# One head per 2 MB tile in place of two heads per 4 MB tile, in an attention-gradient kernel at the DMA limit

## The chip, the cores and the metric

The kernel runs on one core of one Trainium2 chip. The metric is the device time of the whole program in microseconds (us), lower is better; a time quoted here is the median of a kernel's runs, with the lowest and highest in brackets. The core computes with five engines: TensorE (PE, matrix products; its weight loads are counted apart as PEld), VectorE (DVE), ScalarE (ACT), GpSimd (POOL) and SyncE (SP). Its data travels through 16 DMA engines between the main memory (HBM) and the on-chip memory.

 "Same" means within 2%.

## The reference

For each of 64 heads (2 batches of 32) there is one query row of 128 numbers and 8192 rows of K and V; all data is bf16. The outputs are the attention output and the three gradients:

```python
B, H, Sq, Sk, D = 2, 32, 1, 8192, 128
def _fwd_reference(q, k, v):
    scale = q.shape[-1] ** -0.5
    scores = jnp.einsum("bhqd,bhkd->bhqk", q, k) * scale
    p = _softmax(scores, axis=-1)
    return jnp.einsum("bhqk,bhkd->bhqd", p, v)

def reference(q, k, v, grad_out):
    out, vjp = jax.vjp(_fwd_reference, q, k, v)
    return (out, *vjp(grad_out))            # out, dq, dk, dv
```

K and V of one head are 2 MB each, so 268.4 MB must be read. The gradients dK and dV have the same shapes, so 268.4 MB must be written. All other data is tiny.

## The kernel before

The kernel keeps six 4 MB tiles, each holding K or V of two heads. A tile has 128 partitions of 128 rows, which is 32 KB per partition. `load` fills a tile with one DMA of 4 MB. The program then advances in slots; in a slot a sixteen-row chunk of a tile is transposed on PE, copied to on-chip memory by ACT, and used for scores on PE. Later slots form the products with the weights (`acc`) and the gradient (`outer`). A gradient is written over the tile it came from, and is stored by one DMA of 4 MB when the last chunk is done; the last pair is stored in smaller pieces.

```python
GH = 2                                   # heads in a tile
NTILE = 6
...
    NT = GH * Sk // P                    # 128 rows in a partition
    NCH = NT // CH                       # 8 chunks in a tile
    SL = 2 * NCH                         # 16 slots for a pair of heads
    load_eng = nc.sync
    store_eng = nc.gpsimd
...
    def load(i, w, pieces=(NCH,)):
        t = kvp.tile([P, NT, D], BF16, tag=f"kv{slot_of(i, w)}", name="kvt")
        src = (v_v if w else k_v)[i]
        c = 0
        for m in pieces:
            n0, n1 = c * CH, (c + m) * CH
            pin(load_eng.dma_start(out=t[:, n0:n1, :], in_=src[:, n0:n1, :]))
            c += m
...
    def outer(i, w, c, ends):            # gradient of one chunk, in place
        pin(nc.vector.tensor_tensor(out=h.tile[w][:, n0 : n0 + CH, :] ..., op=ALU.mult))
        if c + 1 in ends:
            at = ends.index(c + 1)
            b0, b1 = (ends[at - 1] if at else 0) * CH, (c + 1) * CH
            dst = (dv_v if w else dk_v)[i]
            pin(store_eng.dma_start(out=dst[:, b0:b1, :], in_=h.tile[w][:, b0:b1, :]))

    A1 = NCH + 4; O1 = A1 + 1; A0 = A1 + NCH; O0 = A0 + 1
    whole = [NCH]
    last_v = [NCH // 2, NCH]
    last_k = [NCH // 2, NCH - 2, NCH - 1, NCH]
    for g in range(SL * NP + O0 + NCH + 4 - SL):
        if (i := at(O1 + NCH)) is not None and i + 3 < NP:
            load(i + 3, 0)
        if (i := at(O0 + NCH)) is not None and i + 3 < NP:
            load(i + 3, 1)
        if x := within(O1):
            outer(x[0], 1, x[1], last_v if x[0] == NP - 1 else whole)
        ...
            ev = transpose_chunk(i, r)   # 16 transposes on PE, one copy on ACT
        ...
            score_chunk(*prev)           # 16 score products on PE
```

The cuts are marked with `...`.

## Time and profile before

| before | value | where it is read |
|---|---|---|
| time | 1307.86 us (1306.82 to 1308.02), 3 runs | the timed runs |
| profiled span | 1310.5 us | first line of the page |
| PE / ACT / DVE busy | 88% / 75% / 65% | first part of the page |
| loads + stores, share of the DMA engines | 49.5% + 48.2% | queue table |
| rate at 200–400 us, at 600–800 us | 427, 413 GB/s | windows |

These lines are from the profile page of the kernel before: the busy time of each engine with its instruction count, the mean busy share of the 16 DMA engines (in tenths) and the rate they moved in 40 equal slices of the span, the DMA queues (packets, MB, share of 16 engines' span), and two kinds of DMA with the median time from issue to landing in us. Loads are q1 and stores are q0.

```profile
PE 1147.5 (88%) x19108; PEld 849.1 (65%) x19108; DVE 850.5 (65%) x1551; ACT 984.3 (75%) x641; POOL 37.4 (3%) x76
...
DMA  9999999999999999999999999999999999999968
GB/s 399 429 374 429 427 429 427 429 428 428 427 424 417 429 422 421 413 415 418 414 413 412 411 417 420 413 417 419 403 421 411 421 408 414 425 404 423 414 257 348
...
q1 hardware_dynamic: 9968, 268.51, 49.5%
q0 software_dynamic: 9792, 268.44, 48.2%
q8 instruction: 149, 2.44, 0.7%
...
out_dram<-kvt POOLq DMA_DIRECT2D x62, 4096.0 KB, 40.2
kvt<-in_v_dram SPq DMA_DIRECT2D x32, 4096.0 KB, 27.8
```

The DMA row is nine tenths or more for 38 of 40 slices while no computing engine is full. The kernel is bound by DMA. The rate is 427 to 429 GB/s at first and about 415 in the second half, at the same busy share.

The windows view of before says it by stretch. Columns: the stretch, its length, busy us of PE, PEld, DVE, ACT and POOL with instruction counts, the granted PE clock, the DMA share and the rate in GB/s.

```profile
60.00:100.00 40.00, 40.00 (x725) 30.01 (x721) 30.90 (x55) 36.72 (x24) 1.06 (x2) 1.00 0.93 384
200.00:400.00 200.00, 178.63 (x2968) 132.21 (x2965) 131.99 (x239) 152.75 (x100) 5.32 (x10) 0.92 1.00 427
600.00:800.00 200.00, 178.48 (x2933) 131.79 (x2929) 129.54 (x236) 150.99 (x99) 4.78 (x9) 0.91 1.00 413
...
1260.00:1270.00 10.00, 8.87 (x129) 6.62 (x131) 3.52 (x7) 6.03 (x5) 0.00 (x0) 0.83 0.33 139
1270.00:1280.00 10.00, 9.93 (x176) 7.10 (x172) 9.28 (x16) 9.50 (x8) 0.53 (x1) 1.00 0.51 215
```

### The profile page before, as it was taken

To read this page: it belongs to the slowest core of one execution; us is meant where nothing else is said; L and a number is where in the kernel's file an instruction comes from. 1 tells how busy PE (TensorE), PEld (TensorE's weight loads), DVE (VectorE), ACT (ScalarE), POOL (GpSimd) and SP (SyncE) were. 2 spreads that over 40 slices of the span, in tenths; PEclk is the share of its full clock that TensorE was granted. 3 is DMA by queue.
4 is the path that set the end of the run, shared out by engine and by line. 5 is a ranking of instruction groups with operands and counts; after the bars stand their busy time and mean duration, and the time that the engine had idled before them with its cause. 6 is when DMAs were issued, how large, how long until landed. Compare 5 with 4: busy or idle time off the path is not lost.

```text
span 1310.5 us, 41375 instructions
## 1 busy us (share of the span) xinstructions
PE 1147.5 (88%) x19108; PEld 849.1 (65%) x19108; DVE 850.5 (65%) x1551; ACT 984.3 (75%) x641; POOL 37.4 (3%) x76
## 2 busy tenths in 40 slices
PE   5999998898988988989889898898998988888894
PEld 4777766676766666666666676666666666666661
DVE  0677875766766767657676675665766757566666
ACT  5999987876877877778777787777876878777770
POOL 0000000000000000000000000000000000000000
PEclk9999998998989989889898898988988989888896
DMA  9999999999999999999999999999999999999968
GB/s 399 429 374 429 427 429 427 429 428 428 427 424 417 429 422 421 413 415 418 414 413 412 411 417 420 413 417 419 403 421 411 421 408 414 425 404 423 414 257 348
DMA packets 19933, 539.58 MB, mean 412 GB/s; under 512 B 2480, under 2 KB 2480, under 8 KB 2992
## 3 DMA queue, kind: packets, MB, share of 16 engines
q1 hardware_dynamic: 9968, 268.51, 49.5%
q0 software_dynamic: 9792, 268.44, 48.2%
q8 instruction: 149, 2.44, 0.7%
q14 instruction: 24, 0.20, 0.0%
HBM read 268.47 MB, written 268.47 MB: 410 GB/s over the span
## 4 chain that ended last, share of the span: by engine, by line
issue 78%; DMA 14%; PE 3%; POOL 2%; DVE 1%; SPq 0%; POOLq 0%; ACT 0%; DVEq 0%; ACTq 0%
DMA kvt<-in_v_dram 11%; DMA out_dram<-kvt 3%; POOL out_dram L446 2%; PE tp L183 1%; DVE kvt L432 1%; PE acc L376 1%; PE dpw L194 1%; POOLq L446 0%; PE sw L194 0%; ACT ev L185 0%; DVE sel L399 0%; SPq L93 0%; SPq L100 0%; PE sw L222 0%; PE acc L413 0%
## 5 line engine op out<-in xcount | busy, mean ns | idle before, releaser
L185 ACT COPY ev<-tp 128x2048 bf16<-128x2048 bf16 x512 | 954.0, 1865 | 293.6 <-PE tp L183 276.1
L183 PE MATMUL tp<-ident_bf,kvt 128*128 128x128 bf16 x8192 | 585.3, 229 | 127.3 <-DMA kvt<-in_k_dram 76.8
L432 DVE TENSOR_TENSOR kvt<-qb,pair 128x2048 bf16<-128x2048 bf16 x512 | 615.3, 1219 | 49.6 <-PE acc L376 46.7
L183 PEld LDWEIGHTS <-kvt 128*128 128x128 bf16 x8192 | 505.1, 103 | 137.2 <-DMA kvt<-in_k_dram 79.1
L194 PEld LDWEIGHTS <-ev 128*128 128x128 bf16 x8192 | 239.9, 96 | 218.0 <-issue 135.4
L376 PE MATMUL acc<-kvt,E_pad 128*64 128x512 bf16 x1024 | 173.1, 421 | 0.0
L376 PE MATMUL acc<-kvt,dS_pad 128*64 128x512 bf16 x1024 | 169.4, 416 | 1.0 <-DVE dS_pad L362 1.0
L194 PE MATMUL sw<-qdT,ev 128*128 128x2 bf16 x4096 | 142.0, 164 | 2.2 <-ACT ev L185 2.2
L194 PE MATMUL dpw<-qdT,ev 128*128 128x2 bf16 x4096 | 142.2, 164 | 1.0 <-ACT ev L185 1.0
L270 DVE CUSTOM_DVE_ANT_0 junk<-E_f,dpw 64x128 bf16<-64x128 f32 x64 | 18.3, 285 | 144.1 <-PE dpw L194 143.7
L207 DVE TENSOR_REDUCE mp<-sw 64x1 f32<-64x128 f32 x64 | 18.5, 289 | 108.5 <-PE sw L194 108.1
L446 POOL DMA_DIRECT2D out_dram<-kvt x68 | 36.3, 534 | 1261.7 <-DVE kvt L432 632.9
L399 DVE SCALAR_TENSOR_TENSOR sel<-acc,diag,sel 128x128 f32<-128x128 f32 x192 | 67.3, 351 | 6.8
L376 PEld LDWEIGHTS <-dS_pad 128*64 128x64 bf16 x1024 | 38.2, 112 | 29.4 <-issue 6.3
L376 PEld LDWEIGHTS <-E_pad 128*64 128x64 bf16 x1024 | 37.7, 112 | 26.8 <-issue 6.5
L262 DVE CAST E_pad<-E_f 64x128 bf16<-64x128 f32 x64 | 15.3, 239 | 48.5 <-ACT E_f L252 48.5
L413 PE MATMUL acc<-par,sel 128*128 128x2 f32 x128 | 22.0, 241 | 8.0 <-DVE sel L399 8.0
L176 DVE CAST qb<-dpw 128x128 bf16<-128x128 f32 x64 | 18.2, 284 | 13.4 <-PE dpw L167 13.4
L413 PEld LDWEIGHTS acc<-par,sel 128*128 128x128 f32 x128 | 19.7, 195 | 9.5 <-DVE sel L399 9.5
L340 DVE TENSOR_SCALAR negdelta<-dpw,rl 128x1 f32<-128x1 f32 x32 | 7.0, 218 | 27.0 <-PE dpw L300 27.0
L252 ACT ACTIVATE E_f<-sw,negm 64x128 f32<-64x128 f32 x64 | 23.2, 362 | 1.6
L352 DVE SCALAR_TENSOR_TENSOR dSu<-dpw,negdelta,E_f 64x128 f32<-64x128 f32 x64 | 22.4, 350 | 2.1
(49 smaller groups left out, 230.1 us busy)
## 6 DMA issues: line engine op xcount, KB each, us to landing
out_dram<-kvt POOLq DMA_DIRECT2D x62, 4096.0 KB, 40.2
kvt<-in_v_dram SPq DMA_DIRECT2D x32, 4096.0 KB, 27.8
kvt<-in_k_dram SPq DMA_DIRECT2D x31, 4096.0 KB, 27.9
out_dram<-kvt POOLq DMA_DIRECT2D x3, 2048.0 KB, 8.7
kvt<-in_k_dram SPq DMA_DIRECT2D x1, 2048.0 KB, 11.5
kvt<-in_k_dram SPq DMA_DIRECT2D x2, 512.0 KB, 4.5
kvt<-in_k_dram SPq DMA_DIRECT2D x1, 1024.0 KB, 6.9
out_dram<-kvt POOLq DMA_DIRECT2D x1, 1024.0 KB, 7.6
```

Of the source, the lines that this page charges most:

```text
L183: pin(nc.tensor.transpose(tp[:, t, :], src[:, c * CH + t, :], ident_bf[:]))
L185: pin(nc.scalar.copy(out=ev[:], in_=tp[:]))
L194: nc.tensor.matmul(dst[:, c * CH + t, :], lhsT=ev[:, t, :], rhs=qdT[:, w, GH * i : GH * (i + 1)], start=True, stop=True,)
L207: pin(nc.vector.reduce_max(out=h.mp[hs], in_=h.s[hs, :, g], axis=AX.X))
L252: nc.scalar.activation(out=h.E_f[hs], in_=h.s[hs, :, g], func=ACT.Exp, bias=h.negm[hs], scale=scale, accum_out=h.ld[hs, g : g + 1],)
L270: nc.vector.tensor_tensor_reduce(out=junk[hs], in0=h.E_f[hs], in1=h.dp[hs, :, g], scale=1.0, scalar=0.0, op0=ALU.mult, op1=ALU.add, accum_ ...
L352: nc.vector.scalar_tensor_tensor(out=dSu[hs], in0=h.dp[hs, :, g], scalar=negdelta[hs], in1=h.E_f[hs], op0=ALU.add, op1=ALU.mult,)
L376: nc.tensor.matmul(h.acc[w][g : g + CW, :], lhsT=wts[:, n0 * GH : n0 * GH + CW], rhs=rows[:, n0 : n0 + QT, :].rearrange("p n d -> p (n d)" ...
L399: nc.vector.scalar_tensor_tensor(out=h.sel[:], in0=block, scalar=diag[:, b : b + 1], in1=h.sel[:], op0=ALU.mult, op1=ALU.add,)
L413: nc.tensor.matmul(h.acc[w][:, 0:GH], lhsT=h.sel[:], rhs=par[:], start=True, stop=True)
L432: nc.vector.tensor_tensor(out=h.tile[w][:, n0 : n0 + CH, :].rearrange("p n (e t) -> p n e t", t=2), in0=h.qb[w][:] .rearrange("p (e t) -> ...
L446: pin(store_eng.dma_start(out=dst[:, b0:b1, :], in_=h.tile[w][:, b0:b1, :]))
```

## The change

A tile holds one head (2 MB, 16 KB per partition), and there are twelve. A head takes 8 slots where a pair took 16, so a head's steps are half as wide and come twice as often. Gradients are written over the tile as before. The first store can go out earlier, transfers are finer, and the last head is stored chunk by chunk. The intent is a shorter fill, a shorter tail and a deeper supply of tiles for the DMA engines. The core of the diff, with cuts marked:

```diff
-GH = 2
-NTILE = 6
+NTILE = 12
...
-    NT = GH * Sk // P
+    NT = Sk // P
...
-    load(0, 0, (1, 1, 2, 4))
+    load(0, 0, (1, 1, 2))
...
-        for g, hs in halves:
-            pin(nc.vector.reduce_max(out=h.mp[hs], in_=h.s[hs, :, g], axis=AX.X))
+        pin(nc.vector.reduce_max(out=h.mp[:], in_=h.s, axis=AX.X))
...      (exponential, weighing and normalising likewise: once per head, no halves)
-                    lhsT=wts[:, n0 * GH : n0 * GH + CW],
+                    lhsT=wts[:, n0 : n0 + CW],
...
-    last_v = [NCH // 2, NCH]
-    last_k = [NCH // 2, NCH - 2, NCH - 1, NCH]
+    last = list(range(1, NCH + 1))
+    AHEAD = NTILE // 2
...
-        if (i := at(O1 + NCH)) is not None and i + 3 < NP:
-            load(i + 3, 0)
+        if (i := at(O1 + NCH)) is not None and i + AHEAD < BH:
+            load(i + AHEAD, 0)
...
-            outer(x[0], 1, x[1], last_v if x[0] == NP - 1 else whole)
+            outer(x[0], 1, x[1], last if x[0] == BH - 1 else whole)
```

## The prediction

> **What bounds the kernel now.** The DMA engines. The page's DMA row is 9 in every slice but the last two; its queue table gives loads 49.5% and stores 48.2% of 16 engines' span. PE is busy 88%, ACT 75%, DVE 65%. While it had prefetched tiles (window 60 to 100 us) PE ran 725 matmuls in 40 us, against 2940 in 200 us later: compute can go about a fifth faster than it is fed. The Trainium skill (DMA: Bandwidth & Descriptors, "Issuing engines are not separate DMA queues") says that queues share the same 16 engines and interleave; the trace agrees, the shares sum to 98%.
>
> My account of one DMA engine's 1310 us, from the packet records:
> - 1024 packets of 32 KB at the median 1213 ns: 1242 us
> - instruction fetch (0.7%): 9 us
> - semaphore packets of 9 ns: 1 us
> - packets slower than the median: about 25 us in loads, 8 in stores, nearly all after 400 us, in the first third of a load, on several engines at once; the windows show 427 GB/s at 200 to 400 us and 413 to 419 later
> - idle: about 18 us in the last 70 us (windows 1260 to 1280: share 0.33 and 0.51; after 1300: 0.59), 3 at the start, 3 around 70 to 80 us (202 and 328 GB/s).
>
> **What the change does.**
> 1. A tile row is 16 KB. The 16 KB packets that exist take 611 ns (loads), so twice 611 less 1213 is 9 ns per 32 KB: +9 us, and +1 for twice the semaphore packets.
> 2. Tail. Now the last load lands about 1261 us, 12.6 MB of stores are left from 1274, and the end comes 50 us after the landing. After, 6.3 MB remain, the last head has half the slots and its stores go out by chunk: 9 to 10 us of idle in place of 18, -8 us. Last landing to end falls to about 35 us.
> 3. Fill. First store near 30 us instead of 55.6; the dip at 70 to 80 us goes: -3 us.
> 4. PE and ACT work is equal (about 80 more matmuls of 19108). DVE gets twice the picks (+90 us at 351 ns each) and half-width softmax steps, off the critical path. A head holds its tiles for 17 and 9 slots of 4 per tile, not 29 and 14 of 8 per tile, so 18 MB are free for transfers in place of 13. DMA is saturated already, so this buys little.
> 5. Twice as many loads begin. If each beginning costs what it does now (25 us over 64 loads), slow packets grow by up to 25 us; if the deeper queue keeps loads back to back, as before 400 us, they shrink. I put +5 us.
>
> Sum: 1308 + 10 - 8 - 3 + 5 = 1312 us. Range 1288 to 1336. Faster by over 2%: 0.07; within 2%: 0.86; slower by over 2%: 0.07.
>
> **What would show it.** DMA row at 9 to the end; median 16 KB packet about 611 ns; load and store shares near 98%; last 70 us with about 10 us of idle; no slice under 400 GB/s at 60 to 100 us; DVE 900 to 950 us, PE and ACT about unchanged; stores over 20 us to landing (queue, not compute).
>
> **What would make it wrong.** Slow packets vanishing (towards 1280) or doubling (1335); per-head chains (maximum, exponential, normalisation, twice as often) stalling PE enough to starve the DMA, seen as DMA share below 0.97 in the middle; 2 MB stores paying a start-up that 4 MB ones hid.

## More of the kernel before

A run has a state. A run over 1.5% above the fastest run of the same kernel is called slow and left out; everything compared here is fast against fast.

The mean share counts an engine as busy when a packet of its is under way, however long that packet takes.

## The result, and the profile after

The kernel after took 1304.59 us (1303.87 to 1304.87, 4 runs), and the kernel before, on the same chip in the same rounds, 1307.94 us (1306.82 to 1308.81, 4 runs). The ratio is 0.9974, 95% interval 0.9957 to 0.9991, which is "same". All ratios here are the mean time of one kernel's fast runs over the mean of the other's in the same rounds, so not quite the ratio of the quoted medians. The predicted 1312 us was 7 us too high and well inside the range. The sum was right; the next sections show that two of its terms had the wrong sign.

The same lines of the page, for the kernel after (span 1303.1 us):

```profile
PE 1154.0 (89%) x19268; PEld 873.0 (67%) x19268; DVE 937.5 (72%) x2122; ACT 974.8 (75%) x641; POOL 72.4 (6%) x142
...
DMA  9999999999999999999999999999999999999965
GB/s 390 423 427 427 427 427 427 428 426 430 427 427 427 427 427 429 427 428 427 429 427 427 429 427 424 418 420 425 421 416 420 419 421 421 418 421 422 394 281 206
...
q1 hardware_dynamic: 19040, 268.51, 48.9%
q0 software_dynamic: 19296, 268.44, 48.7%
q8 instruction: 150, 2.46, 0.7%
...
out_dram<-kvt POOLq DMA_DIRECT2D x126, 2048.0 KB, 40.4
kvt<-in_v_dram SPq DMA_DIRECT2D x64, 2048.0 KB, 49.3
```

The rate now stays at 427 until about 780 us (24 slices) where before lost it after about 400 us, but it falls to 418–421 at last all the same. The end is worse: the last three slices are 394, 281 and 206 GB/s; before had 414, 257 and 348. The same windows of after, and two of the end:

```profile
60.00:100.00 40.00, 39.35 (x702) 30.10 (x702) 34.04 (x79) 35.17 (x23) 2.66 (x5) 1.00 1.01 426
200.00:400.00 200.00, 180.19 (x2946) 135.82 (x2947) 143.91 (x324) 148.68 (x97) 10.62 (x20) 0.92 1.01 428
600.00:800.00 200.00, 178.06 (x2993) 134.58 (x2991) 145.78 (x328) 150.97 (x100) 10.63 (x20) 0.96 1.01 427
800.00:1000.00 200.00, 181.98 (x2990) 137.48 (x2986) 145.00 (x330) 150.62 (x100) 10.10 (x19) 0.92 1.01 420
...
1250.00:1260.00 10.00, 9.97 (x176) 7.99 (x173) 8.29 (x21) 8.78 (x7) 0.53 (x1) 1.00 0.31 128
...
1270.00:1280.00 10.00, 8.70 (x131) 5.89 (x128) 8.54 (x21) 5.33 (x5) 0.67 (x2) 0.95 0.31 126
```

From the packet records, and idle from the windows, one can keep a ledger of the mean DMA engine's span. The slow part is the time of packets beyond the median (1213 ns at 32 KB, 611 ns at 16 KB), summed and divided by 16:

```
us per engine                  before                     after
data packets at the median     1024 x 1.213 = 1242        2048 x 0.611 = 1251
instruction fetch, semaphores  9 + 1                      9 + 2
packets over the median        25.8 loads + 8.6 stores    8.8 loads + 6.5 stores
idle in the last 70 us         18                         28
idle at the start, at 70-80    3 + 3                      3 + 0
sum                            1310                       1308
span                           1310.5                     1303.1
```

The sum of after is 5 us over its span; shares of 1.01 in its windows show that packet times overlap a little, so the ledger is good to about half a per cent. Slow packets shrank by 19 us and the end grew by 10. Why did two things that look unrelated move in opposite directions? The view of the kernel after's DMA at 1254 to 1274 us (each slice 0.5 us) was the first hint. The rows are the share of the engines in tenths, the rate, and the queues with packets, MB and share:

```profile
DMA  0100000099956999920100099579996691000010
GB/s 33 66 0 33 33 33 33 0 524 524 524 229 295 524 524 524 426 98 33 66 33 0 33 524 524 229 295 524 524 524 262 262 524 33 0 33 33 33 33 33
...
q0 software_dynamic: 296, 4.31, 51.4%
q1 hardware_dynamic: 10, 0.13, 1.6%
```

33 GB/s over half a microsecond is 16.5 KB: one packet. For several microseconds at a time a single engine works, packet after packet, and 15 stand idle. Two stores then use all the engines briefly, and again one remains.

**A straggler.** A transfer's completion is recorded in the trace 16 times. The Trainium skill ("DMA: Bandwidth & Descriptors", section "Why a DMA increments its semaphore by 16 and not by 1") explains it: each of up to 16 engines does its share and adds one to the semaphore when its own data has landed. The trace agrees, with 16 landings for each 2 MB transfer. I call *lag* the time from the median of a transfer's 16 landings to the last one. It is worked out from the landings in the trace, which no view lists; times are those of the windows. Lag in us, for sampled transfers:

```
before, stores   1.0 at 74    5.7 at 235   10.8 at 396   15.2 at 557   15-19 from 599 to 1247
after, both      4.9 at 212   12.1 at 536  15.7 at 698   18.3 at 861   22.3 at 1023   25.1 at 1185
```

One of the 16 engines falls behind, in after by about 2% of the time ((25.1 - 4.9) / (1185 - 212) = 0.021), in the stores of before by about 3% until 557 us ((15.2 - 1.0) / (557 - 74) = 0.029). In before its lag stops growing at 15 to 19 us (its loads lag only 3 to 8 us at 200 to 1030 us), at the time when the rate falls to 413 to 417: the other 15 have to wait for it, because a tile is free only when all 16 shares have landed. The waits view of before has SP, which issues the loads, waiting for stores to land (us in total, times, longest):

```profile
SPq L93 <- DMA out_dram<-kvt: 1188.3, 58, 59.9
```

The 28 us of idle at the end of after is close to its last lag, and the 18 us of before to its own. That match is not general: split_rows below ends with a lag of about 40 us and 24 us of idle, quarter_scores with 20 and 25. The reading that the experiments test is that the span is set by the slowest engine, and that its excess is paid either in the middle, when buffers run out, or at the end.

### The profile page after: what moved, and what is told of

Same layout as the page of the kernel before. It is cut to its first block, busy times and chain, and to the rows that moved or that the text cites. A ratio compares the mean times of both kernels' runs of the same rounds, so it can differ in the third digit from the quotient of the medians.

```text
span 1303.1 us, 42566 instructions
## 1 busy us (share of the span) xinstructions
PE 1154.0 (89%) x19268; PEld 873.0 (67%) x19268; DVE 937.5 (72%) x2122; ACT 974.8 (75%) x641; POOL 72.4 (6%) x142
## 3 DMA queue, kind: packets, MB, share of 16 engines
q8 instruction: 150, 2.46, 0.7%
## 4 chain that ended last, share of the span: by engine, by line
issue 80%; DMA 11%; POOL 4%; DVE 2%; PE 1%; POOLq 0%; SPq 0%; DVEq 0%
DMA kvt<-in_v_dram 8%; POOL out_dram L390 4%; DMA out_dram<-kvt 3%; DVE kvt L376 1%; PE tp L166 1%; POOLq L390 0%; PE acc L321 0%; DVE sel L344 0%; PE dpw L177 0%; SPq L89 0%; SPq L96 0%; DVE sel L338 0%; PE sw L177 0%; PE acc L358 0%; DVE pair L252 0%
## 5 line engine op out<-in xcount | busy, mean ns | idle before, releaser
L177 PE MATMUL dpw<-qdT,ev 128*128 128x1 bf16 x4096 | 140.9, 164 | 12.0 <-DVE qb L159 10.7
L344 DVE SCALAR_TENSOR_TENSOR sel<-acc,diag,sel 128x128 f32<-128x128 f32 x384 | 134.6, 351 | 13.6
L177 PE MATMUL sw<-qdT,ev 128*128 128x1 bf16 x4096 | 142.5, 164 | 1.1 <-ACT ev L168 1.1
L390 POOL DMA_DIRECT2D out_dram<-kvt x134 | 71.3, 532 | 1219.2 <-DVE kvt L376 1186.8
L358 PE MATMUL acc<-ones,sel 128*128 128x1 f32 x256 | 43.3, 239 | 6.2 <-DVE sel L344 6.2
L264 PE MATMUL dpw<-ld,ones 128*128 128x1 f32 x256 | 46.3, 250 | 0.1
L338 DVE TENSOR_SCALAR sel<-acc,diag 128x128 f32<-128x128 f32 x128 | 44.0, 344 | 0.0
L358 PEld LDWEIGHTS acc<-ones,sel 128*128 128x128 f32 x256 | 39.0, 193 | 7.3 <-DVE sel L344 7.3
L159 DVE CAST qb<-dpw 128x128 bf16<-128x128 f32 x128 | 35.4, 277 | 6.0 <-PE dpw L150 6.0
L264 PEld LDWEIGHTS dpw<-ld,ones 128*128 128x128 f32 x256 | 38.2, 188 | 0.5 <-DVE ld L235 0.5
## 6 DMA issues: line engine op xcount, KB each, us to landing
out_dram<-kvt POOLq DMA_DIRECT2D x126, 2048.0 KB, 40.4
```

Source lines behind the costliest of these rows:

```text
L159: pin(nc.vector.tensor_copy(out=h.qb[w][:], in_=h.qbp))
L177: nc.tensor.matmul(dst[:, c * CH + t : c * CH + t + 1], lhsT=ev[:, t, :], rhs=qdT[:, w, i : i + 1], start=True, stop=True,)
L264: nc.tensor.matmul(out, lhsT=ones[:].to_broadcast([P, P]), rhs=col, start=True, stop=True)
L338: nc.vector.tensor_scalar(out=h.sel[:], in0=block, scalar1=diag[:, 0:1], scalar2=None, op0=ALU.mult)
L344: nc.vector.scalar_tensor_tensor(out=h.sel[:], in0=block, scalar=diag[:, b : b + 1], in1=h.sel[:], op0=ALU.mult, op1=ALU.add,)
L358: nc.tensor.matmul(h.acc[w][:, 0:1], lhsT=h.sel[:], rhs=ones[:], start=True, stop=True)
```

## The experiments

Two theories stood after the first look. **Depth**: the change supplied the engines with more transfers at once, and so kept packets fast. **Packet size**: packets of 16 KB behave better than packets of 32 KB. The lag added a third, the **straggler**: one engine needs more time for its sixteenth of the data, and the other two only say where that is paid. Then the question is what makes it slow; the candidates were the software-built descriptors of the stores, an engine that is always slow, and the compute instructions. All kernels were run in groups on one chip with the kernel before beside them; "before there" is its median in the group. Four kernels give wrong results where said.

### 1. Packets of 16 KB in the kernel before: split_rows

```diff
-            pin(load_eng.dma_start(out=t[:, n0:n1, :], in_=src[:, n0:n1, :]))
+            for a, b in ([(n0, n1)] if m < NCH else [(0, NT // 2), (NT // 2, NT)]):
+                pin(load_eng.dma_start(out=t[:, a:b, :], in_=src[:, a:b, :]))
```

Stores are split the same way; all else is the kernel before.

> The kernel before, with every 4 MB transfer issued as two of 2 MB (each row in two 16 KB packets); tiles, slots and buffering unchanged. If packet size is a cost of its own (9 ns per 32 KB) and the better middle of the changed kernel comes from its deeper queue: 1316 to 1320 us, and the middle windows still fall from about 427 to 410-417 GB/s after 400 us. If the better middle comes from the smaller transfers themselves: 425 GB/s or more after 400 us and 1305 us or less.

Measured: 1300.37 us (1299.74 to 1302.96), ratio 0.9952 (0.9935 to 0.9968), before there 1306.26. It is, with its variant split_early (section 11), the fastest correct kernel. Windows of split_rows:

```profile
200.00:400.00 200.00, 176.45 (x3051) 131.16 (x3050) 136.78 (x245) 156.97 (x102) 10.63 (x20) 0.97 1.01 427
600.00:800.00 200.00, 176.52 (x2944) 130.08 (x2942) 132.30 (x236) 151.70 (x100) 10.63 (x20) 0.94 1.01 421
800.00:1000.00 200.00, 172.81 (x2929) 128.07 (x2927) 133.56 (x239) 150.82 (x99) 10.10 (x19) 0.96 1.01 419
```

The rate in the middle rises from before's 413 to 421 with the same six tiles of 4 MB. That is between the two rates expected (410 to 417, or 425 and more), while the time is that of the second. Halving the transfers alone gives at least the change's gain (0.9952 against 0.9974; the intervals overlap). The lag did not go away: stores lagged 16.8 us at 546, 27 at 870 and 39.3 at 1194.

### 2. Fewer tiles in the kernel after: depth8

```diff
-NTILE = 12
+NTILE = 8
```

> The changed kernel with 8 tiles in place of 12 (10 MB free for transfers by slot count, less than the 13 of the kernel before). Theory: one DMA engine is about 2% slower than the other 15; its lag grows until the buffers are used up and then all wait for it, so depth decides only when the rate falls and how long the straggler works alone at the end. Then: the rate falls earlier than in the kernel before (under 420 GB/s from about 300 us), the lag (last of a transfer's 16 landings minus their median) stops at 10-15 us, idle in the last 70 us is under 20 us, and the total stays within 1% of the changed kernel (1300 to 1317). Rival, small transfers run better and depth is not needed: 427 GB/s in the middle and 1295 or less. Rival, depth is what feeds the DMA: 1330 or more.

Measured: 1311.34 us (1307.25 to 1314.89), ratio 1.0036 (1.0008 to 1.0065). Windows of depth8:

```profile
200.00:400.00 200.00, 181.91 (x2972) 136.97 (x2970) 144.65 (x326) 150.39 (x100) 10.63 (x20) 0.92 1.01 425
600.00:800.00 200.00, 182.69 (x2983) 137.68 (x2984) 144.00 (x326) 150.13 (x99) 10.63 (x20) 0.92 1.01 415
800.00:1000.00 200.00, 173.14 (x2948) 131.25 (x2945) 142.29 (x324) 149.16 (x100) 10.63 (x20) 0.97 1.01 416
```

With 16 MB of tiles in place of 24 the rate falls at about 300 us, not 780, and the lag of the stores stops at 17 to 25 us, where I had expected 10 to 15. The tail has less idle time in turn (13 us in the last 70; about 420 GB/s until 1270 us). Depth moves the place of the loss; taking away a third of the tiles cost about 0.6% of the time (1.0036 against 0.9974, from different rounds; two of the four runs took 1307 to 1308 us, the profiled one among them, and two 1314 to 1315). PE was as busy as with twelve tiles at 600 to 800 us (182.7 and 178.1 us), so compute did not limit it.

### 3. Stores with descriptors made in hardware: act_stores

```diff
-    store_eng = nc.gpsimd
+    store_eng = nc.scalar
+    pending = []
...
-            pin(store_eng.dma_start(out=dst[:, b0:b1, :], in_=h.tile[w][:, b0:b1, :]))
+            pending.append((dst[:, b0:b1, :], h.tile[w][:, b0:b1, :]))
...      (end of each slot)
+        for dst, src in pending:
+            pin(store_eng.dma_start(out=dst, in_=src))
+        pending.clear()
```

> The changed kernel with its stores issued from ScalarE (hardware descriptors) in place of GpSimd (software descriptors), at the end of the same slot. If the straggler is slow because of the software queue: lag under 5 us throughout, 427 GB/s until 1200 us, total 1270 to 1287. If the straggler is slow for another reason (instruction fetch, its path to memory): lag grows to about 25 us as in the changed kernel and the total is 1298 to 1310. If ScalarE's waits starve PE: ACT shows new waits on DVE and the DMA share falls under 0.97 in the middle.

Measured: 1315.82 us (1315.51 to 1316.28), ratio 1.0072 (1.0057 to 1.0087). The lag stayed (about 20 us in loads at 1135, up to 27 in stores), so the software queue is not what makes the engine slow. The kernel was slower for another reason as well: ACT, now also the issuer of stores, stood once for 24.7 us, and the window 1200 to 1230 moved only 292 GB/s at a DMA share of 0.77. The waits view of act_stores (engine, line, what it waited for: us in total, times, longest):

```profile
ACT ev L169 <- DMA kvt<-in_k_dram: 24.7, 1, 24.7
```

A copy on ACT has no need of a load to land. I put the wait down to completion semaphores: in this trace loads and stores use the same eight, in after each had eight of its own. No run isolates that.

### 4. No compute at all: copy_only

Loads and stores with the order and tiles of the kernel after, and nothing between them; the result is wrong.

```diff
-        pin(nc.vector.tensor_tensor(out=h.tile[w][:, n0 : n0 + CH, :] ..., op=ALU.mult))
...
-            ev = transpose_chunk(i, r)
-        ...                       (all other steps of the slot removed as well)
+    nc.vector.memset(dqT[:], 0.0)
+    nc.vector.memset(oT[:], 0.0)
```

> Wrong results on purpose: the changed kernel's loads and stores alone, V and K stored back as loaded; software stores kept, almost no instruction stream. If the software queue makes the straggler: lag still grows by about 2% (20 us or more at the end), total 1280 to 1295. If instruction fetch makes it: no lag (under 5 us), total 1262 to 1272. Either way it is the floor of this pattern of transfers.

Measured: 1255.39 us (1255.32 to 1255.44), ratio 0.9609, 431 GB/s from 200 to 1000 us in the windows. The lag was at most 2 us. So no DMA engine is slow by itself under these loads and stores; the time is even below both ranges that I gave. It takes the compute to make one slow, and that costs the kernel after 1304.6 - 1255.4 = 49 us, some fifteen times what the change gained (3.3 us).

### 5 and 6. Compute of one kind: copy_dve and copy_pe

Both add compute to copy_only, on tiles that have nothing to do with the transfers except DVE's in-place product, and both give wrong results. copy_dve has the 512 in-place products on DVE and 512 copies on ACT: many bytes, few instructions. copy_pe has 36 transposes of one constant tile per slot on PE: many instructions, no data of the transfers.

```diff
 copy_dve
+            pin(nc.vector.tensor_tensor(out=h.tile[w][...], in0=qbc[...], in1=prc[...], op=ALU.mult))
+            ev = evp.tile([P, CH, P], BF16, tag="ev", name="ev")
+            pin(nc.scalar.copy(out=ev[:], in_=tpc[:]))
 copy_pe
+        for t in range(36):
+            pin(nc.tensor.transpose(tpc[:, t % CH, :], ident_bf[:], ident_bf[:]))
```

> Wrong results on purpose: the loads and stores alone, plus the 512 in-place products on DVE and 512 copies from PSUM on ACT, about 1100 instructions with the real kernel's SBUF traffic. Theory F: fewer than 10 fetch packets, lag under 3 us, 1255 to 1265 (the wait for DVE before a store can cost a little at the end). Theory B: lag of 10 us or more, total over 1270.

> Wrong results on purpose: the loads and stores alone, as in copy_only, plus about 19100 transposes of a constant tile on PE that wait for nothing and touch no loaded tile (36 per slot). Theory F, instruction fetch makes the straggler: some 150 fetch packets appear again, the lag (last of 16 landings minus their median) grows to 20 us or more and the total is 1268 to 1295. Theory B, the compute engines' traffic in SBUF makes it: lag under 3 us and 1253 to 1258 as copy_only.

Measured on one chip: copy_dve 1256.78 us (1256.42 to 1257.80), ratio 0.9617; copy_pe 1299.33 us (1298.94 to 1299.76), ratio 0.9942; that time is 4 us above the range that I gave. The DMA view of copy_dve at 300 to 400 us:

```profile
DMA packets 2952, 43.10 MB, mean 431 GB/s; under 512 B 320, under 2 KB 320, under 8 KB 320
...
q0 software_dynamic: 1478, 21.59, 50.5%
q1 hardware_dynamic: 1471, 21.48, 50.2%
q14 instruction: 3, 0.02, 0.1%
```

And of copy_pe:

```profile
DMA packets 2933, 42.71 MB, mean 427 GB/s; under 512 B 326, under 2 KB 326, under 8 KB 326
...
q1 hardware_dynamic: 1503, 21.89, 51.2%
q0 software_dynamic: 1415, 20.58, 48.6%
q8 instruction: 14, 0.23, 0.9%
```

The line to see is q8, the instruction fetch, which copy_dve does not have. PE's instructions alone bring back nearly all of the loss: 1299.33 - 1256.78 = 42.6 us, and the lag with it (33.8 us in the loads at the end; at most 3.4 in copy_dve). copy_pe's rate also falls from 427 to 420 GB/s at 800 to 1000 us, although PE reads no transferred byte and no transfer waits for PE. On-chip traffic of ACT and DVE costs 1.4 us against copy_only (1256.78 against 1255.39, different chips).

The packet records show what happens. In copy_pe, at 100 to 800 us, about 165 packets per 100 us take 615 to 699 ns in place of 611. Together they cover 105 us per 100 us, which is one engine's whole time, and 91% of them begin within 15 ns of the end of the slow packet before: it is one engine, nearly all of whose packets are slow while PE works. In copy_only and copy_dve there are at most 27 such packets per 100 us. The records do not name the engine of a packet, so that the series and the late landing are the same engine is inferred.

The fetch packets are not what slows that engine. A fetch packet begins as another packet ends, so the records tell whose turn it took. At 94 of the 98 fetches in these 700 us only packets of the usual 611 ns ended just then (of the other four, three had no such packet and one had both kinds). So the fetches fell on the other engines. Each took about 1 us, and the packet after it some 400 ns more. Nor are slow packets more frequent beside a fetch: 22% of them overlap one, where chance would give 23%. The number of q8 packets follows PE's instructions; the slowness goes with these instructions in another way.

An estimate from the same records closes the sum. The excess of the slow packets is 4.33 us per 100 us in copy_pe, 4.22 in after (at 100 to 700 us) and 2.93 in quarter_scores below (at 100 to 1000 us): 1.2 to 1.4 ns for each matmul or weight load of PE. Taken over all of them, all counted as the straggler's, and added to 2048 packets of 611 ns (1251 us), it gives 1297, 1305 and 1289 us for the straggler alone. The spans were 1297.1, 1303.1 and 1288.2.

A count check: the Trainium skill ("Runtime: NRT & Kernel Launch", section "Instruction fetch mechanics") says that an engine's instructions are fetched in blocks of 16 KiB, 256 instructions, and that the cost of crossing one is "mostly hidden". The trace agrees with the block: 150 packets in after, times 256, are 38,400, and PE has 2 x 19268 = 38,536 matmuls and weight loads. On PE's side the cost is indeed hidden: in copy_pe PE was busy for 200.00 of 200 us at 200 to 400 us. The loss of 42.6 us over 147 fetch packets is 0.29 us for each 256 instructions; the DMA engines pay it, but not through the fetch packets themselves.

### 7. A third fewer PE instructions in the full kernel: quarter_scores

One score product of four equal columns replaces four products. The result is wrong.

```diff
-        for t in range(CH):
+        for t in range(0, CH, 4):
...
-                    dst[:, c * CH + t : c * CH + t + 1],
+                    dst[:, c * CH + t : c * CH + t + 4],
...
-                    rhs=qdT[:, w, i : i + 1],
+                    rhs=qdT[:, w, i : i + 1].to_broadcast([P, 4]),
```

> Wrong results on purpose: the changed kernel with one score matmul in place of four (it writes four equal columns), 12288 of PE's 38500 instructions fewer, transfers unchanged. Theory F: fetch packets fall from 150 to about 102, the lag near 1200 us from 25 to about 17 us and the total from 1304.6 to 1290-1298. Theory B, or PE's own time as a bound: lag unchanged at 25 us and 1300 to 1306 (B), or a drop by more than 20 us (PE).

Measured: 1292.29 us (1289.79 to 1295.27), ratio 0.9895 (0.9865 to 0.9925). The page of quarter_scores has the fetch packets, and its windows the rate:

```profile
q8 instruction: 102, 1.67, 0.5%
```

```profile
200.00:400.00 200.00, 161.46 (x2050) 115.32 (x2050) 143.72 (x326) 148.83 (x100) 10.38 (x20) 0.92 1.01 428
800.00:1000.00 200.00, 160.10 (x2050) 114.23 (x2050) 146.24 (x333) 149.41 (x101) 10.66 (x20) 0.93 1.01 429
```

Against the kernel after it has 48 fewer fetch packets and 12.3 us less time (medians of different rounds; its four runs lay at 1290 and 1295), 0.26 us for each 256 instructions, close to the 0.29 of copy_pe. The rate does not fall in the middle any more, and the lag is about 19.9 us at 1231 in place of 25.1 at 1185. So the dose and the effect go together in the full kernel too. PE's busy time fell as well, but in copy_only and copy_pe the time moved with PE's instructions while nothing waited for PE.

### 8. Which engine is it: probe

The kernel after with ten tiles, so that room is left, and sixteen tiny loads of 1 to 16 rows, issued from 1085 to 1120 us.

```diff
-NTILE = 12
+NTILE = 10
...
+        if g == SL * 52 + 6:
+            for n in range(1, 17):
+                pr = const.tile([16, D], BF16, name=f"probe{n}")
+                pin(load_eng.dma_start(out=pr[:n, :], in_=k_v[0][:n, 0, :]))
```

> The changed kernel with 10 tiles, and 16 tiny loads of 1, 2, ... 16 rows of 256 bytes, issued one after the other on the load queue at about 1060 us. A load of n rows should use n of the 16 DMA engines, the first n. The landing time then jumps by the lag (10 to 20 us) at the n that first includes the straggler, and stays there; if it does not jump at one n, the rows are not spread so, or no single engine lags.

The Trainium skill (the same page and section on the 16 increments) says that such a load of n rows uses the n lowest-numbered engines. The trace agrees on the number: n rows, n landings of data. Measured (one look, 1312.45 us, state unknown, result correct): the loads of 1 to 4 rows landed at 1098.5 to 1099.1 us. With 5 rows, four landings came at 1098.5 to 1099.3 and the fifth at 1115.5. With 6 rows, five came at 1098.7 to 1099.5 and one at 1116.9. The jump at 5 says that the straggler is the fifth engine, with 16.3 us of queue in front of it. The loads of 7 to 16 rows were held up by SP's own waits, but each of them again had one landing 3 to 12 us after all its others, that of 16 rows too: no second engine of the 16 lagged like that.

### 9. The last head stored whole: whole_last

```diff
-    last = list(range(1, NCH + 1))
+    last = whole
```

> The changed kernel with the last head's gradients stored whole, not by chunk. My prediction gave the shorter tail 8 us. If the tail's idle is idle of the 15 other engines while the straggler works off its lag, storing by chunk matters only after the last product: 0 to 4 us (1304 to 1309). If the prediction's reading was right, most of the 8 us is lost: 1310 or more.

Measured: 1304.03 us (1303.79 to 1306.17), ratio 0.9962 (0.9942 to 0.9981); the kernel after has 1304.59 and 0.9974. Storing the last head chunk by chunk, a part of the change meant for the tail, gains nothing. The page's last slices are 395, 287 and 215 GB/s; in after they are 394, 281 and 206. On this reading the tail waits for the straggler's backlog, and finer stores do not shorten that.

### 10, 11 and 12. Size, number or order of the transfers: split_parts, split_early, split_swap

split_rows had changed three things at once: packets of 16 KB, twice as many transfers, and first halves that land earlier. Each kernel here changes a different part. split_parts also issues two transfers of 2 MB, of 64 partitions each, so its packets stay 32 KB. split_early stores the first half of a gradient four slots sooner. split_swap is split_rows with the later half of a tile loaded first, so no first half lands earlier.

```diff
 split_parts (before; stores alike)
+            for a in range(2 if m == NCH else 1):
+                rows = slice(a, P, 2) if m == NCH else slice(0, P)
+                pin(load_eng.dma_start(out=t[rows, n0:n1, :], in_=src[rows, n0:n1, :]))
 split_early (loads of split_rows)
-    whole = [NCH]
+    whole = [NCH // 2, NCH]
 split_swap (split_rows)
-            for a, b in ([(n0, n1)] if m < NCH else [(0, NT // 2), (NT // 2, NT)]):
+            for a, b in ([(n0, n1)] if m < NCH else [(NT // 2, NT), (0, NT // 2)]):
```

> The kernel before with every 4 MB transfer issued as two of 64 rows (even and odd partitions), so 2 MB each as in split_rows but packets stay 32 KB. If the straggler's own work sets the time, the 9 ns per 32 KB saved against split_rows (1024 pairs on the straggler, 9 us) shows: 1290 to 1296 us. If packet size does not matter for the total, 1299 to 1302 as split_rows. If half the rows make a worse use of the memory ports, packets of 32 KB are slower than 1213 ns and it is over 1305.

> split_rows with the first half of every gradient tile stored as soon as its four products are done, four slots earlier. If split_rows is already at what the straggler needs (copy_pe: 1299 us), nothing moves: 1298 to 1302. If finer hand-over is what made split_rows faster, more of it gives 1296 or less.

> split_rows with the two halves of every load issued in the other order, so that the first transpose of a tile waits for the half issued last and the early start on half a tile is lost; packets stay 16 KB, reloads wait for both stored halves as in split_rows. If the gain of split_rows over the kernel before is its smaller packets: 1299 to 1303 us. If it is the early start: 1307 to 1316, with load packets slower again after 400 us and the middle at 410-417 GB/s. Between 1303 and 1307: both.

| kernel | time, us | ratio (95%) | before there |
|---|---|---|---|
| split_parts | 1315.44 (1312.07 to 1317.88) | 1.0045 (1.0026 to 1.0065) | 1309.61 |
| split_early | 1301.33 (1300.33 to 1302.81) | 0.9938 (0.9915 to 0.9961) | 1309.61 |
| split_swap | 1303.12 (1302.42 to 1306.41) | 0.9967 (0.9954 to 0.9979) | 1306.97 |
| split_rows, again | 1300.37 (1299.74 to 1302.96) | 0.9952 (0.9935 to 0.9968) | 1306.26 |

Twice the transfers with 32 KB packets gained nothing and lost half a per cent. That is in line with the Trainium skill ("DMA: Bandwidth & Descriptors", section "Rules for kernel authors"), which says of two transfers to disjoint partition halves "Don't bother". The time of load packets over the median was 34.1 us per engine, against 25.8 in before. With 16 KB packets, and no earlier landing, split_swap keeps most of the gain: 0.33 of 0.48 per cent. The rest is at the edge of the noise, as the intervals overlap. Storing earlier gained nothing that can be told from split_rows. So the runs point to the packet size. They do not isolate it: split_parts also interleaves partitions, which split_swap does not.

## Why the prediction was right

It was right in its sum, by errors that cancelled, and partly for wrong reasons. "Bound by DMA" held, and the account of the mean engine's time was a correct ledger. What it missed is that the time is not set by the mean engine, but by the slowest.

- **Step 1, +10 us for 16 KB packets: right as arithmetic.** The median packet took 611 ns, the ledger's line rose from 1242 to 1251 us. As a judgement of packet size it was wrong: split_rows pays the same price and is 0.48% faster in all, with a higher rate in the middle (421 against 413 GB/s at 600 to 800 us).
- **Step 2, -8 us in the tail: this step failed.** I expected 10 us of idle in the last 70 us in place of 18, and there were 28, so +10. The geometry was about right. In the chain that ended last, the last load of before was issued at 1226.77 and took 34.31 us, which leaves 49 us to the end at 1310.5; that of after leaves 38, where I had said 35:

```profile
1226.77 34.31 DMA kvt<-in_v_dram
```

```profile
1215.54 49.35 DMA kvt<-in_v_dram
```

  But I took the idle for a matter of few bytes left and long compute steps. It is the time in which 15 engines are done and one still has its backlog: a load of 2 MB took 49 us to land, about 25 of them lag. whole_last shows that the stores by chunk bought nothing.
- **Step 3, -3 us in the fill: right.** The window at 60 to 100 us rose from 384 to 426 GB/s, worth 40 x (426 - 384) / 426 = 4 us.
- **Step 4, compute equal and off the critical path: right.** PE went from 1147.5 to 1154.0 us, ACT from 984.3 to 974.8, DVE from 850.5 to 937.5 (I said 900 to 950), and stores still took 40.4 us to land. "DMA is saturated already, so this buys little" was true of the total: depth decides when the 15 begin to wait, and depth8 put its cost at about 0.6% for a third of the tiles.
- **Step 5, +5 us of slow packets: this step failed too, with the opposite sign.** Slow packets shrank by 19 us (34.4 to 15.3). I had named that outcome among the risks and weighed it too low. I had taken slow packets for a cost of beginning a load. I now read them as the trace of 15 engines that ran dry while they waited for the sixteenth, and of the sixteenth's own slowness; only the second part is shown. With finer packets and more tiles free, more of the lag could run on to the end (depth8 shows the reverse: fewer tiles, an earlier fall and 13 us of idle in the tail). That is how I read the tail's +10 us.

In one sum: 1308 + 10 (packets, semaphores) + 10 (tail) - 4 (fill) - 19 (slow packets) = 1305, and 1304.6 was measured. Steps 2 and 5 missed by +18 and -24 us, and they are tied together. Had I treated them as one account, the straggler's excess, I would have had a reason for "same".

**What is shown and what stays open.** Shown: one of 16 engines falls behind by 2 to 3% in before and after; PE's instruction stream is enough to cause it; fewer PE instructions shrink it; it is neither the software queue, nor the bytes that ACT and DVE move, nor fetch packets on that engine. Open: what it is that goes with each PE instruction and slows that one engine. The runs also report their span and clock, so I can't say that any of them was free of the recording of instructions, and that recording is a candidate. Open as well: why 32 KB packets suffer more beside the straggler.

## What to carry to other kernels

When DMA is at its limit, look at the spread of the 16 landings of a transfer before explaining a rate or a tail with means: an idle tail and a sagging middle can be one debt paid at two places, and moving it changes the time little. Cutting PE instructions (0.26 to 0.29 us for each 256) paid here although PE was not the bottleneck, and a plain split of each 4 MB transfer into two with 16 KB packets (1300.4 us, ratio 0.9952) was worth at least as much as the whole restructuring (0.9974). A sum that comes out right is no proof of its terms: check each term against the trace after.

## What the Trainium skill lacked or had wrong

- **"DMA: Bandwidth & Descriptors", section "Latency and other measured facts".** It names engines 7 and 15 as usually slower, with the software queue's descriptor rings as its best guess. Here the slow one was the fifth engine (landings jump from 1099.1 to 1115.5 us when a load takes a fifth row), in one look. One engine stayed slow with hardware descriptors (lag about 20 us in act_stores), and none was slow without PE's instructions (lag at most 2 us in copy_only, 3.4 in copy_dve).
- **"Runtime: NRT & Kernel Launch", section "Instruction fetch mechanics".** The page does not say what a fetch costs the DMA engine that carries it: in copy_pe a fetch packet took about 1 us and the packet after it some 400 ns more. Nor has it the larger cost that goes with PE's instructions in a kernel bound by DMA (copy_pe against copy_dve, 42.6 us, 0.29 us for each 256), which is not the fetch packets' own and whose origin is open.
- **"CRC Debugging", section "Comparing the Two Runs".** It gives queue 14 for instruction refill. The trace has most of it under queue 8 (150 packets, 2.46 MB, in after) and only 31 packets under queue 14.
- **"Perfetto Trace Analysis", section "Identifying the Most-Contended Engine".** It calls occupancy misleading for the 16 DMA engines, but no page names the spread of a transfer's 16 landings as the place to see that one engine lags. The mean share was 1.00 in before at 200 to 400 us and at 600 to 800 us, while the rate fell from 427 to 413 GB/s.
- **No page has it:** smaller packets may be better beside a straggler. 16 KB packets gave 0.9952 and 0.9967 (split_rows, split_swap), 32 KB in the same number of transfers 1.0045 (split_parts), though split_parts also interleaves partitions.
